# Attention, top-1 experts and a rational-activation MLP on one core: building the token table in two passes

## The chip, the cores and the metric

The kernel runs on one core of a Trainium2 chip. The metric is the time of one execution in device microseconds, from the first to the last instruction of that core and what lies around it. The engines are TensorE (PE), VectorE (DVE), ScalarE (ACT), GpSimd (POOL) and SyncE (SP), each with its own queue; SP and POOL issue the DMAs of the stretch that matters here.

## The reference, cut to what matters

```
x   = linear_attention(q, k, v)            # (8, 8, 576, 64) -> tokens N = 4608, D = 512
keep = x @ w_skip > 0                       # other tokens pass unchanged
e    = argmax(x[keep] @ w_gate)             # one of 8 experts per kept token
g    = softmax(x[keep] @ w_gate)[e]
x[keep] += g * (relu(x[keep] @ w1[e]) @ w2[e])       # w1: 512 x 1024, w2: 1024 x 512
h   = x @ w_in                              # w_in: 512 x 2048, w_out: 2048 x 512
out = P(h) / Q(h) @ w_out                   # cubic over quadratic in |h|, elementwise
```

## The kernel before

There are three stages. Attention (`attention`, eight batches) writes the tokens to `xd` in DRAM and keeps the router's logits in SBUF. The experts (`experts`) read them, and `mlp` does the last two products in blocks of 384 tokens. Products in float32 are made of three passes over a high and a low half, so weights and activations are first split: ScalarE copies the high half, VectorE or GpSimd subtracts to get the low one.

The experts work in up to 25 slots of 256 tokens, each slot of one expert; a slot has two halves of 128, so there are `NH` = 50 columns of token indices `sidx` (128 x 50), one per half. The change lies in how `sidx` comes about and who waits for it.

`positions` gives every token a place. `token_table` (L696) turns places into `sidx` in four chunks of 12, 12, 8 and 4 token columns. In each chunk VectorE compares (`hh`, which of the 50 columns), compares (`lh`, which of the 128 rows) and multiplies by the token number (`tg`); PE adds a matmul for each token column into the PSUM tile `ptab`. Two more VectorE instructions (`high`, `sidx`) finish all 50 columns. After the first chunk `slot_table` finds the expert of each slot (`etab`), and SP issues the four loads of the first expert's `w1`. After the table `kind_table` says for each slot how many halves have tokens and whether the next slot has another expert (`kind`, `change`).

Then, in program order (L985 to L996): POOL gathers slot 0's rows (`gather(0)`, two indirect DMAs), issues two loads of `w2`, and gathers slot 1's rows (`gather(1)`). VectorE and ScalarE split the first four of `w1`'s eight column groups, `gate_sum` and `gate_out` store the last tokens' gates to `gd` (many small pieces), PE transposes slot 0's rows, these are split, then the rest of `w1`.

A slot (L911) runs under a branch on `kind`. Slot 0 first splits `w2` (ScalarE the high halves, VectorE and GpSimd in turn the low ones) and gathers its gates. In `part1_full` (L885) PE does layer 1 in four blocks `f2` of 24 matmuls; ScalarE and VectorE make `hh` and `hl` of each (`relu`). In slot 0 `tables()` follows: `next_table`, the loads of the next expert's weights, `pair_table`. PE goes on with the transposes of the next slot's rows and with layer 2 of half 1, whose result is scaled, added and scattered back. After the branch come `gather(i + 2)` and layer 2 of half 0.

Instructions of one engine run in the order of its queue. That order is the code's within each block written with `manual_schedule`; between blocks the compiler may bring work forward (it does so with `gather(2)` in slot 0), but not into or out of a branch that it depends on.

Of the kernel before, what the change touches and what calls it, by code (L numbers as in the profile page):

```python
# [10 lines left out]
I32 = mybir.dt.int32  # L11
# [47 lines left out]
@with_exitstack  # L59
def tile_attention_moe_moe2(ctx: ExitStack, tc: tile.TileContext, q, k, v, w_skip, w_gate, w1, w2, w_in, w_out, ca, cb, out, dbg=None):  # L60
    nc = tc.nc
    nc.scalar.preload_act_table_set("natural_log_exp_and_others")
    const = ctx.enter_context(tc.tile_pool(name="const", bufs=1))
    ident = const.tile([P, P], F32, name="ident")
    make_identity(nc, ident)
    ones = const.tile([P, 2], F32, name="ones")
    nc.vector.memset(ones, 1.0)
    wg = const.tile([P, 4, E + 1], F32, name="wg")
    av = const.tile([P, 4], F32, name="av")
    bv = const.tile([P, 2], F32, name="bv")  # L70
    ab = const.tile([P, 2], F32, name="ab")
    qc = const.tile([P, 1], F32, name="qc")
    nc.vector.memset(qc, 1.0 + 1e-6)
    sidx = const.tile([P, NH], I32, name="sidx")
    gates = const.tile([P, NH], F32, name="gates")
    etab = const.tile([1, 32], I32, name="etab")
    xtab = const.tile([1, 32], I32, name="xtab")
    kind = const.tile([1, 32], I32, name="kind")
    change = const.tile([1, 32], I32, name="change")
    pair = const.tile([1, 3, 32], I32, name="pair")  # L80
    early = const.tile([1, 33], I32, name="early")
    xd = tc.dram_tile([NT, DM], F32, name="xd")
    gd = tc.dram_tile([NT, 1], F32, name="gd")
    wc_in = tc.dram_tile([DM, F2], F32, name="wc_in")
    wc_out = tc.dram_tile([F2, DM], F32, name="wc_out")

    with ExitStack() as rst:
        rc = rst.enter_context(tc.tile_pool(name="r_const", bufs=1))
        logits = rc.tile([P, NC, E + 1], F32, name="logits")
        R = dict(pair=pair, early=early) | routing_tiles(rc)  # L90
        attention(tc, q, k, v, w_gate, w_skip, ca, cb, ident, ones, wg, av, bv, ab, logits, xd, gd, R)
        if dbg is not None and "logits" in dbg:
            nc.sync.dma_start(out=dbg["logits"], in_=logits)
            nc.sync.dma_start(out=dbg["xd"], in_=xd)
            return
        with tc.tile_pool(name="hold", bufs=1, side="right", reuse_waits="tile") as hp:
            hold = hp.tile([P, DM // P * F1], F32, name="hold")
            hs = ExitStack()
            ahead = []
            experts(tc, w1, w2, w_in, w_out, wc_in, wc_out, xd, gd, ident, logits, sidx, gates, etab, xtab, kind, change, pair, early, hold, ahead, hs, R, dbg)  # L100
            if dbg is not None and "sidx" in dbg:
                return
            rst.close()
            if dbg is not None and "x2" in dbg:
                nc.sync.dma_start(out=dbg["x2"], in_=xd)
                nc.sync.dma_start(out=dbg["wi"], in_=wc_in)
                nc.sync.dma_start(out=dbg["wo"], in_=wc_out)
                return
            mlp(tc, xd, wc_in, wc_out, av, ab, qc, ident, hold, ahead, out)
            hs.close()  # L110
# [62 lines left out]
def attention(tc, q, k, v, w_gate, w_skip, ca, cb, ident, ones, wg, av, bv, ab, logits, xd, gd, R):  # L173
    nc = tc.nc
    with ExitStack() as st:
        inp = st.enter_context(tc.tile_pool(name="a_in", bufs=3))
        tails = st.enter_context(tc.tile_pool(name="a_tail", bufs=3))
        work = st.enter_context(tc.tile_pool(name="a_work", bufs=2))
# [209 lines left out]

        def tn(b, j):
            if j == 0:  # L390
                T["xs", b] = work.tile([P, J, DM], F32, name="xs")
            if j == J:
                T["xt", b] = work.tile([P, DM], F32, name="xt")
            xout = T["xs", b][:, j, :] if j < J else T["xt", b]
            if j in ON_ACT and b < B - 1:
                for g in range(H):
                    nc.scalar.activation(xout[:, g * D:(g + 1) * D], T["px", b, j][:, g // 2, (g % 2) * D:(g % 2 + 1) * D], AF.Identity, scale=T["rq", b][:, j, g // 2, g % 2:g % 2 + 1])
                return
            nc.vector.tensor_tensor(out=xout.rearrange("p (r h d) -> p r h d", r=4, h=2), in0=T["px", b, j][:, :, 0:2 * D].rearrange("p r (h d) -> p r h d", h=2),
                                    in1=T["rq", b][:, j].unsqueeze(3).to_broadcast([P, 4, 2, D]), op=ALU.mult)  # L400
# [292 lines left out]
    nc.vector.tensor_copy(out=pair[:, 0], in_=done[:, 1, 32:64])  # L693


def token_table(tc, p, ps, R, sidx):  # L696
    nc = tc.nc
    tok, posb = R["tok"], R["posb"]
    lh = p.tile([P, P, NC], BF16, name="lh")
    ptab = ps.tile([P, 2, NH], F32, name="ptab")  # L700
    c0 = 0
    for n in (CG, CG, 8, 4):
        cs = slice(c0, c0 + n)
        hh = p.tile([P, CG, NH], BF16, name="hh", bufs=2)[:, 0:n]
        tg = p.tile([P, CG, 2, NH], BF16, name="tg", bufs=2)[:, 0:n]
        nc.vector.tensor_tensor(out=hh, in0=R["rowh"].unsqueeze(1).to_broadcast([P, n, NH]), in1=posb[:, 1, cs].unsqueeze(2).to_broadcast([P, n, NH]), op=ALU.is_equal)
        nc.vector.tensor_tensor(out=lh[:, :, cs], in0=R["rowx"][:, :, 0:n], in1=posb[:, 0, cs].unsqueeze(1).to_broadcast([P, P, n]), op=ALU.is_equal)
        nc.vector.tensor_tensor(out=tg, in0=hh.unsqueeze(2).to_broadcast([P, n, 2, NH]),
                                in1=tok.rearrange("p m c -> p c m")[:, cs].unsqueeze(3).to_broadcast([P, n, 2, NH]), op=ALU.mult)
        for c in range(c0, c0 + n):  # L710
            nc.tensor.matmul(out=ptab, lhsT=lh[:, :, c], rhs=tg[:, c - c0], start=(c == 0), stop=(c == NC - 1))
        c0 += n
        yield
    high = p.tile([P, NH], F32, name="high")
    nc.vector.tensor_scalar(out=high, in0=ptab[:, 0, :], scalar1=64.0, scalar2=float(NOWHERE), op0=ALU.mult, op1=ALU.add)
    nc.vector.tensor_tensor(out=sidx, in0=high, in1=ptab[:, 1, :], op=ALU.add)
    yield


def experts(tc, w1, w2, w_in, w_out, wc_in, wc_out, xd, gd, ident, logits, sidx, gates, etab, xtab, kind, change, pair, early, hold, ahead, hs, R, dbg=None):  # L720
    nc = tc.nc
    KD, KF = DM // P, F1 // P
    ET = mybir.EngineType
# [2 lines left out]
    with ExitStack() as st:  # L726
# [151 lines left out]
            load_w2(e)  # L878

        def tables():  # L880
            next_table(tc, R, xtab)
            load_next(0)
            pair_table(tc, R, sidx, change, pair, early)

        def part1_full(i, hh, hl):  # L885
            for f2 in range(KF // 2):
                relu(f2, layer1(i, f2), hh, hl)
            if i == 0:
                tables()
            pts = [transposes(i + 1, a) for a in range(2)] if i < MAXS - 1 else []  # L890
            py = layer2(1, hh, hl)
            for a, pt in enumerate(pts):
# [3 lines left out]
        def part1_half(i, hh, hl):  # L896
            last = i == MAXS - 1
            r = []
            for g in range(2):
                r.append(layer1_half(i, g))  # L900
            pts = []
            for g in range(2):
                split_half(g, turn_half(g, r[g]), hh, hl)
# [1 line left out]
                    pts.append(transposes(i + 1, g))  # L905
            for a, pt in enumerate(pts):
                split_x(i + 1, a, pt)
            if i == 0:
                tables()

        def slot(i, kd, ch):  # L911
            last = i == MAXS - 1
# [10 lines left out]
            with full.Else():  # L923
                with tc.manual_schedule():
                    part1_half(i, hh, hl)
            with tc.manual_schedule():
                if i + 2 < MAXS:
                    gather(i + 2)
# [33 lines left out]
        with tc.manual_schedule():  # L962
# [6 lines left out]
            gate_exp(tc, R, c1, NC)  # L969
            with tc.tile_pool(name="r_ps", bufs=1, space=PSUM, reuse_waits="tile") as rps:  # L970
                positions(tc, rps, R)
                tt = token_table(tc, rp, rps, R, sidx)
                next(tt)
                slot_table(tc, R, etab)
                e0 = expert(etab, 0, [ET.SP, ET.Pool])
                for c in range(4):
                    load_w1(e0, c=c, n=4)
                for _ in range(4):
                    next(tt)
                kind_table(tc, R, sidx, kind, change)  # L980
            pp = st.enter_context(tc.tile_pool(name="e_ps", bufs=1, space=PSUM, reuse_waits="tile"))
            ps["t"] = [pp.tile([P, KD, P], F32, name=f"pt{a}") for a in range(2)]
            ps["h"] = [pp.tile([P, 2 * SLOT], F32, name=f"ph{f2}") for f2 in range(KF // 2)]
# [1 line left out]
            gather(0)  # L985
            for c in range(2):
                load_w2(e0, nc.gpsimd, c, 2)
            gather(1)
            for c in range(W1A):
                split_w1(c, False)  # L990
            gate_sum(tc, R, c1, NC)
            gate_out(tc, R, gd, (B // 2 - 1,))
            for a in range(2):
                split_x(0, a, transposes(0, a))
            for c in range(W1A, 8):
                split_w1(c, False)  # L996
            if dbg is not None and "sidx" in dbg:
                next_table(tc, R, xtab)
                for nm, t in (("sidx", sidx), ("etab", etab), ("kind", kind[:, 0:MAXS]), ("xtab", xtab)):
                    nc.sync.dma_start(out=dbg[nm], in_=t)  # L1000
                return
        with tc.manual_schedule():
            kd, ch = get(kind, 0, 2), get(change, 0, 2)
        with tc.If(kd > 0):
            slot(0, kd, ch)
        rs.close()
        ap_ = hs.enter_context(tc.tile_pool(name="ahead", bufs=1, side="right", reuse_waits="tile"))
        ahead.extend(ap_.tile([P, KD, AHEAD * P], F32R, name=f"wi{m}") for m in "hl")
# [205 lines left out]
```

## Time and profile before

| | |
|---|---|
| Time, median of 3 runs (lowest, highest) | 1399.22 us (1395.91, 1400.88) |
| The profiled execution, its span | 1394.98 us, 1393.3 us |
| PE, PE weight loads | busy 1320.0 us (95%), 1195.8 us (86%) |
| DVE, ACT, POOL | busy 1099.6 us (79%), 890.4 us (64%), 296.5 us (21%) |
| Attention | up to about 153 us |
| Routing and slot 0's rows | about 153 to 181 us |
| Experts, from layer 1 of slot 0 | about 181 to 550 us |
| MLP | from about 567 us |

Busy time is the time in which an engine executes; an engine that is busy 95% of the span leaves little room, but only in the stages where it is. The timeline lists the instructions of an engine in order of time, with the idle time just before each in brackets and what ended it; neighbours of one kind are merged (x4 means four of them). "PEclk" is the TensorE clock that was granted, as a share of full speed.

### The profile page before, as it was taken

Reading aid. Unit: us, or ns where it says so; the run is one execution under the profiler, and the core shown is the slowest. Engines: PE = TensorE matmul, PEld = TensorE weight load, DVE = VectorE, ACT = ScalarE, POOL = GpSimd, SP = SyncE. Lnnn points to the kernel's source line nnn. Section 1 sums busy time; section 2 is a strip of 40 time slices with the busy share of each in tenths; the row PEclk is TensorE's granted clock in tenths of the full one; section 3 lists DMA queues with packets and bytes.
Section 4 is the critical chain, followed back from the end, with each engine's and each line's share of the span. In section 5 each row is a group of like instructions: output and inputs, shape, how many; then the busy total and the mean of one; then the engine's idle time right before and its main releaser. Section 6 shows DMA issues by size and latency. Waiting matters only on the chain.

```text
span 1393.3 us, 22173 instructions
## 1 busy us (share of the span) xinstructions
PE 1320.0 (95%) x7470; PEld 1195.8 (86%) x7470; DVE 1099.6 (79%) x2093; ACT 890.4 (64%) x1726; POOL 296.5 (21%) x247
## 2 busy tenths in 40 slices
PE   4999489999899999799999999999999999999998
PEld 3989378888898898789999999999999999999997
DVE  6998754764646565699888888888888888888887
ACT  2655235544242422699787878787877787878786
POOL 5756044556343452241000000000000000000000
PEclk9999689999999999899999999999999999999999
DMA  9984455667646654421000000000000000000000
GB/s 280 320 277 145 129 131 198 230 220 260 229 151 232 239 179 147 139 91 61 23 23 24 23 24 23 23 24 23 24 23 23 24 23 24 23 24 24 1 23 23
DMA packets 86929, 143.82 MB, mean 103 GB/s; under 512 B 21925, under 2 KB 52645, under 8 KB 85745
## 3 DMA queue, kind: packets, MB, share of 16 engines
q1 hardware_dynamic: 79696, 125.88, 27.1%
q0 software_dynamic: 7072, 16.06, 3.8%
q8 instruction: 70, 1.15, 0.4%
q14 instruction: 91, 0.74, 0.2%
HBM read 110.66 MB, written 35.15 MB: 105 GB/s over the span
## 4 chain that ended last, share of the span: by engine, by line
PE 55%; DVE 2%; issue 1%; ACT 1%; DMA 1%; POOL 0%; POOLq 0%; ACTq 0%; DVEq 0%
PE ph L1106 27%; PE py L1151 27%; DMA xd<-y,sidx 1%; PE pt L1090 1%; DVE gl L1132 0%; DVE qq L1130 0%; DVE r L1134 0%; DVE qq L1136 0%; DVE pn L1140 0%; DVE pn L1138 0%; ACT qq L1121 0%; ACT m L1119 0%; DVE pn L1141 0%; POOL x L792 0%; ACT gh L1115 0%
## 5 line engine op out<-in xcount | busy, mean ns | idle before, releaser
L1151 PE MATMUL py<-woh,gl 128*128 128x512 f32 x576 | 227.5, 395 | 0.1
L1151 PE MATMUL py<-woh,gh 128*128 128x512 f32 x576 | 227.4, 395 | 0.0
L1151 PE MATMUL py<-wol,gh 128*128 128x512 f32 x576 | 226.9, 394 | 0.0
L1115 ACT CAST gh<-pn 128x384 fp32r<-128x384 f32 x192 | 98.7, 514 | 142.5 <-PE py L1151 137.2
L1132 DVE TENSOR_TENSOR gl<-pn,gh 128x384 fp32r<-128x384 f32 x192 | 110.1, 573 | 69.5 <-ACT gh L1115 69.3
L1121 ACT ACTIVATE qq<-m,ab 128x384 f32<-128x384 f32 x192 | 136.4, 711 | 6.4
L1106 PE MATMUL ph<-xh,wi0h 128*128 128x384 f32 x384 | 129.6, 338 | 0.3 <-DVE pn L1141 0.2
L1106 PE MATMUL ph<-xh,wi0l 128*128 128x384 f32 x384 | 129.7, 338 | 0.0
L1106 PE MATMUL ph<-xl,wi0h 128*128 128x384 f32 x384 | 129.0, 336 | 0.0
L1151 PEld LDWEIGHTS py<-woh,gl 128*128 128x128 f32 x576 | 108.0, 188 | 24.4 <-DVE gl L1132 1.2
L813 PE MATMUL ph<-xth,w1h 128*128 128x256 f32 x416 | 120.4, 289 | 6.8 <-ACT cvs L743 6.0
L1123 ACT ACTIVATE pn<-ph,av 128x384 f32<-128x384 f32 x192 | 125.5, 653 | 0.0
L1141 DVE SCALAR_TENSOR_TENSOR pn<-pn,av,ph 128x384 f32<-128x384 f32 x192 | 118.1, 615 | 6.8
L1151 PEld LDWEIGHTS py<-wol,gh 128*128 128x128 f32 x576 | 108.2, 188 | 17.8
L1151 PEld LDWEIGHTS py<-woh,gh 128*128 128x128 f32 x576 | 108.3, 188 | 17.5 <-ACT gh L1115 0.6
L1136 DVE TENSOR_TENSOR qq<-m,qq 128x384 f32<-128x384 f32 x192 | 106.8, 556 | 17.7 <-issue 3.9
L813 PE MATMUL ph<-xtl,w1h 128*128 128x256 f32 x416 | 120.0, 288 | 0.1
L813 PE MATMUL ph<-xth,w1l 128*128 128x256 f32 x416 | 119.8, 288 | 0.0
L1138 DVE SCALAR_TENSOR_TENSOR pn<-pn,av,r 128x384 f32<-128x384 f32 x192 | 117.3, 611 | 0.1
L1126 ACT ACTIVATE r<-qq,qc 128x384 f32<-128x384 f32 x192 | 115.9, 604 | 0.0
L1130 DVE SCALAR_TENSOR_TENSOR qq<-qq,r 128x384 f32<-128x384 f32 x192 | 108.7, 566 | 0.0
L1134 DVE SCALAR_TENSOR_TENSOR r<-qq,r 128x384 f32<-128x384 f32 x192 | 106.9, 557 | 0.0
(231 smaller groups left out, 3225.1 us busy)
## 6 DMA issues: line engine op xcount, KB each, us to landing
hold<-in_moe_w_dram SPq DMA_DIRECT2D x8, 2048.0 KB
w2s<-in_moe_w_dram SPq DMA_DIRECT2D x8, 2048.0 KB
hold<-xd SPq DMA_DIRECT2D x12, 768.0 KB
out_dram<-o SPq DMA_DIRECT2D x36, 256.0 KB
vm<-in_v_dram SPq DMA_DIRECT2D x8, 1024.0 KB
qm<-in_q_dram SPq DMA_DIRECT2D x8, 1024.0 KB
xd<-xs SPq DMA_DIRECT2D x8, 1024.0 KB
raw<-in_moe_w_in_dram SPq DMA_DIRECT2D x16, 512.0 KB
```

The lines of the kernel that those rows point to most:

```text
L813: nc.tensor.matmul(out=ph[:, u, :], lhsT=a[:, k, fs], rhs=b[:, k, :], start=(n == 0), stop=(n == 3 * KD - 1))
L1106: nc.tensor.matmul(out=ph, lhsT=w[:, k, :], rhs=x[:, k, :], start=(n == 0), stop=(n == 3 * KD - 1))
L1121: nc.scalar.activation(qq, m, AF.Identity, scale=ab[:, 1:2], bias=ab[:, 0:1])
L1123: nc.scalar.activation(pn, ph, AF.Identity, scale=av[:, 3:4], bias=av[:, 2:3])
L1126: nc.scalar.activation(r2, T[("q",) + second], AF.Ln, bias=qc)
L1130: nc.vector.scalar_tensor_tensor(out=q3, in0=q3, scalar=1.0 + 1e-6, in1=r3, op0=ALU.add, op1=ALU.mult)
L1132: GL(nc).tensor_tensor(out=gl, in0=pn4, in1=gh.bitcast(F32), op=ALU.subtract)
L1134: nc.vector.scalar_tensor_tensor(out=r3, in0=q3, scalar=2.0, in1=r3, op0=ALU.subtract, op1=ALU.mult, reverse0=True)
L1136: nc.vector.tensor_tensor(out=qq, in0=m, in1=qq, op=ALU.mult)
L1138: nc.vector.scalar_tensor_tensor(out=p3, in0=p3, scalar=av[:, 0:1], in1=r3, op0=ALU.add, op1=ALU.mult)
L1141: nc.vector.scalar_tensor_tensor(out=pn, in0=pn, scalar=av[:, 1:2], in1=ph, op0=ALU.add, op1=ALU.mult)
L1151: nc.tensor.matmul(out=py, lhsT=g[:, ts_], rhs=w[:, f, :], start=(f == 0 and n == 0), stop=(f == KF - 1 and n == 2))
```

## The change

Columns 0 and 1 (slot 0) get a pass of their own through all four chunks. `token_table` becomes `table_part` (one chunk for the columns h0 to h1) and `table_end`. The first pass runs before `slot_table`; `first_kind` finds slot 0's `kind` from its two columns. For the other 48 columns, chunks 0 and 1 stand behind the issue of slot 0's gather and of `w2`, ahead of `gate_sum`; chunks 2 and 3 stand in `tables()`, with `gather(1)` and `kind_table` behind them. `tables()` moves from behind all four blocks of layer 1 to behind the second (f2 == 1). Their sums go to the PSUM tile of layer 2's half 0. `lh` is made once, in the first pass. Slot 0's `change` is read behind its branch. Two column groups of `w1` instead of four are split before slot 0's rows. In attention the output tiles `xs` and `xt` move to a pool of their own, allocated first.

```diff
 def attention(...)
+        res = st.enter_context(tc.tile_pool(name="a_res", bufs=2))
...
-                T["xs", b] = work.tile([P, J, DM], F32, name="xs")
+                T["xs", b] = res.tile([P, J, DM], F32, name="xs")
...
-                T["xt", b] = work.tile([P, DM], F32, name="xt")
+                T["xt", b] = res.tile([P, DM], F32, name="xt")
...
+CHUNKS = (CG, CG, 8, 4)
+
+def table_part(nc, p, R, lh, ptab, m, h0, h1):
+    tok, posb = R["tok"], R["posb"]
+    nh, c0, n = h1 - h0, sum(CHUNKS[:m]), CHUNKS[m]
+    cs = slice(c0, c0 + n)
+    hh = p.tile([P, CG, nh], BF16, name=f"hh{h0}", bufs=2)[:, 0:n]
+    tg = p.tile([P, CG, 2, nh], BF16, name=f"tg{h0}", bufs=2)[:, 0:n]
+    nc.vector.tensor_tensor(out=hh, in0=R["rowh"][:, h0:h1].unsqueeze(1).to_broadcast([P, n, nh]), in1=posb[:, 1, cs].unsqueeze(2).to_broadcast([P, n, nh]), op=ALU.is_equal)
+    nc.vector.tensor_tensor(out=tg, in0=hh.unsqueeze(2).to_broadcast([P, n, 2, nh]),
+                            in1=tok.rearrange("p m c -> p c m")[:, cs].unsqueeze(3).to_broadcast([P, n, 2, nh]), op=ALU.mult)
+    if h0 == 0:
         nc.vector.tensor_tensor(out=lh[:, :, cs], in0=R["rowx"][:, :, 0:n], in1=posb[:, 0, cs].unsqueeze(1).to_broadcast([P, P, n]), op=ALU.is_equal)
+    for c in range(c0, c0 + n):
+        nc.tensor.matmul(out=ptab, lhsT=lh[:, :, c], rhs=tg[:, c - c0], start=(c == 0), stop=(c == NC - 1))
+
+def table_end(nc, p, ptab, sidx, h0, h1):
+    high = p.tile([P, h1 - h0], F32, name=f"high{h0}")
     nc.vector.tensor_scalar(out=high, in0=ptab[:, 0, :], scalar1=64.0, scalar2=float(NOWHERE), op0=ALU.mult, op1=ALU.add)
+    nc.vector.tensor_tensor(out=sidx[:, h0:h1], in0=high, in1=ptab[:, 1, :], op=ALU.add)
+
+def first_kind(tc, R, sidx, kind0):
+    nc = tc.nc
+    occ = R["occ"][:, 0:2]
+    nc.vector.tensor_scalar(out=occ, in0=sidx[0:1, 0:2], scalar1=float(NT), scalar2=None, op0=ALU.is_lt)
+    nc.vector.tensor_tensor(out=kind0, in0=occ[:, 0:1], in1=occ[:, 1:2], op=ALU.add)
...
         def tables():
+            for m in range(2, len(CHUNKS)):
+                table_part(nc, rest["p"], R, rest["lh"], rest["ptab"], m, 2, NH)
+            table_end(nc, rest["p"], rest["ptab"], sidx, 2, NH)
+            gather(1)
+            kind_table(tc, R, sidx, kind, change)
             next_table(tc, R, xtab)
...
                 relu(f2, layer1(i, f2), hh, hl)
-            if i == 0:
-                tables()
+                if i == 0 and f2 == 1:
+                    tables()
...
                     part1_half(i, hh, hl)
+            if i == 0:
+                ch = get(change, 0, 2)
...
                 positions(tc, rps, R)
-                tt = token_table(tc, rp, rps, R, sidx)
-                next(tt)
+                lh = rp.tile([P, P, NC], BF16, name="lh")
+                ptab = rps.tile([P, 2, 2], F32, name="ptab")
+                for m in range(len(CHUNKS)):
+                    table_part(nc, rp, R, lh, ptab, m, 0, 2)
                 slot_table(tc, R, etab)
+                table_end(nc, rp, ptab, sidx, 0, 2)
                 e0 = expert(etab, 0, [ET.SP, ET.Pool])
                 for c in range(4):
                     load_w1(e0, c=c, n=4)
-                for _ in range(4):
-                    next(tt)
-                kind_table(tc, R, sidx, kind, change)
+                first_kind(tc, R, sidx, kind0)
...
             gather(0)
             for c in range(2):
                 load_w2(e0, nc.gpsimd, c, 2)
-            gather(1)
-            for c in range(W1A):
-                split_w1(c, False)
+            rest = dict(p=rp, lh=lh, ptab=ps["y"][0][:, 0:2 * (NH - 2)].rearrange("p (m h) -> p m h", m=2))
+            for m in range(2):
+                table_part(nc, rp, R, lh, rest["ptab"], m, 2, NH)
             gate_sum(tc, R, c1, NC)
             gate_out(tc, R, gd, (B // 2 - 1,))
+            for c in range(W1A // 2):
+                split_w1(c, False)
             for a in range(2):
                 split_x(0, a, transposes(0, a))
-            for c in range(W1A, 8):
+            for c in range(W1A // 2, 8):
                 split_w1(c, False)
+            nc.vector.memset(kind, 0)
...
-            kd, ch = get(kind, 0, 2), get(change, 0, 2)
+            kd = get(kind0, 0, 2)
```

In `part1_half`, which a slot of one filled half takes, `tables()` moves ahead of the second transposes in the same way.

## Rows read from the trace of the kernel before

**Rows 1.** Timeline of VectorE: start us, us, engine line op out<-in, idle before.
```profile
158.41 0.78 DVE L706 TENSOR_TENSOR hh<-r_rowh,r_posb 128x600 bf16<-128x600 bf16 x1
161.28 0.96 DVE L707 TENSOR_TENSOR lh<-r_rowx,r_posb 128x1536 bf16<-128x1536 bf16 x1 [2.10 <-DMA xd<-xt]
162.16 1.40 DVE L708 TENSOR_TENSOR tg<-hh,r_tok 128x1200 bf16<-128x1200 bf16 x1
163.47 0.41 DVE L650 TENSOR_TENSOR r_cand<-r_rows,r_cum 1x256 f32<-1x256 f32 x1
...
164.55 0.77 DVE L706 TENSOR_TENSOR hh<-r_rowh,r_posb 128x600 bf16<-128x600 bf16 x1
...
167.43 0.56 DVE L706 TENSOR_TENSOR hh<-r_rowh,r_posb 128x400 bf16<-128x400 bf16 x1
167.92 0.67 DVE L707 TENSOR_TENSOR lh<-r_rowx,r_posb 128x1024 bf16<-128x1024 bf16 x1
168.52 0.97 DVE L708 TENSOR_TENSOR tg<-hh,r_tok 128x800 bf16<-128x800 bf16 x1
...
169.70 0.41 DVE L707 TENSOR_TENSOR lh<-r_rowx,r_posb 128x512 bf16<-128x512 bf16 x1
170.03 0.56 DVE L708 TENSOR_TENSOR tg<-hh,r_tok 128x400 bf16<-128x400 bf16 x1
...
171.42 0.21 DVE L716 TENSOR_TENSOR sidx<-high,ptab 128x50 int32<-128x50 f32 x1
```

**Rows 2.** Timeline of GpSimd, gathers and loads ahead of slot 0 and in it.
```profile
172.51 1.53 POOL L792 DMA_INDIRECT x<-xd,sidx  x1 [34.82 <-DMA hold<-in_moe_w_dram]
174.34 1.28 POOL L792 DMA_INDIRECT x<-xd,sidx  x1 [0.30 <-issue]
175.63 1.62 POOL L775 DMA_DIRECT2D w2s<-in_moe_w_dram  x2
...
191.13 1.10 POOL L873 DMA_INDIRECT gates<-gd,sidx  x1 [11.16 <-DMA gd<-r_gate]
...
196.16 5.02 POOL L780 TENSOR_TENSOR w2l<-w2s,w2h 128x512 fp32r<-128x512 f32 x4
```

**Rows 3.** Timeline of TensorE, transposes, layer 1 and layer 2 of slot 0.
```profile
178.96 1.11 PE L798 MATMUL pt<-ident,x 128*128 128x128 f32 x4 [1.08 <-DMA x<-xd,sidx]
180.74 0.58 PE L813 MATMUL ph<-xth,w1h 128*128 128x256 f32 x1 [0.68 <-ACT xth L778]
...
187.18 0.28 PE L813 MATMUL ph<-xth,w1h 128*128 128x256 f32 x1
...
196.24 0.48 PE L829 MATMUL py<-w2h,hh 128*128 128x512 f32 x1
```

**Rows 4.** Timeline of SyncE's queue, the DMAs that it issues.
```profile
146.31 1.30 SPq L610 DMA_DIRECT2D gd<-r_gate  x2
...
153.46 0.34 SPq L409 DMA_DIRECT2D xd<-xs  x1
...
165.36 2.12 SPq L770 DMA_DIRECT2D hold<-in_moe_w_dram  x4
175.37 0.37 SPq L608 DMA_DIRECT2D gd<-r_gate  x1
...
203.71 0.38 SPq L770 DMA_DIRECT2D hold<-in_moe_w_dram  x1
```

**Rows 5.** Windows: stretch, its us, busy us (x instructions), PEclk granted, DMA share, GB/s.
```profile
168.00:170.00 2.00, 1.17 (x15) 1.10 (x14) 2.00 (x4) 0.99 (x2) 0.00 (x0) 0.50 1.07 349
```

**Rows 6.** Timeline of ScalarE, the copies of the second half of w2.
```profile
192.56 2.18 ACT L778 CAST w2h<-w2s 128x512 fp32r<-128x512 f32 x4 [0.42 <-DMA w2s<-in_moe_w_dram]
```

**Rows 7.** Timeline of VectorE inside slot 0.
```profile
195.34 1.89 DVE L820 SCALAR_TENSOR_TENSOR hl<-ph,hh 128x512 fp32r<-128x512 f32 x3 [0.39 <-issue]
...
198.26 3.20 DVE L660 SCALAR_TENSOR_TENSOR r_cand<-r_cand,r_cum 1x256 f32<-1x256 f32 x1
...
201.94 0.41 DVE L662 TENSOR_TENSOR r_cand<-r_nend,r_cum 1x256 f32<-1x256 f32 x1
```

More of the change, by code (lines that the diff above doesn't have):

```diff
@@ L79, in tile_attention_moe_moe2 @@
     change = const.tile([1, 32], I32, name="change")
+    kind0 = const.tile([1, 1], I32, name="kind0")
     pair = const.tile([1, 3, 32], I32, name="pair")
@@ L99, in tile_attention_moe_moe2 @@
             ahead = []
-            experts(tc, w1, w2, w_in, w_out, wc_in, wc_out, xd, gd, ident, logits, sidx, gates, etab, xtab, kind, change, pair, early, hold, ahead, hs, R, dbg)
+            experts(tc, w1, w2, w_in, w_out, wc_in, wc_out, xd, gd, ident, logits, sidx, gates, etab, xtab, kind0, kind, change, pair, early, hold, ahead, hs, R, dbg)
             if dbg is not None and "sidx" in dbg:
@@ L693, in pair_table @@
     nc.vector.tensor_copy(out=pair[:, 0], in_=done[:, 1, 32:64])
-def token_table(tc, p, ps, R, sidx):
-    nc = tc.nc
[L698 to L717, printed above, removed]
@@ L720, in experts @@
-def experts(tc, w1, w2, w_in, w_out, wc_in, wc_out, xd, gd, ident, logits, sidx, gates, etab, xtab, kind, change, pair, early, hold, ahead, hs, R, dbg=None):
+CHUNKS = (CG, CG, 8, 4)
[9 more added lines that the diff above has]
+    if h0 == 0:
+        nc.vector.tensor_tensor(out=lh[:, :, cs], in0=R["rowx"][:, :, 0:n], in1=posb[:, 0, cs].unsqueeze(1).to_broadcast([P, P, n]), op=ALU.is_equal)
+    for c in range(c0, c0 + n):
+        nc.tensor.matmul(out=ptab, lhsT=lh[:, :, c], rhs=tg[:, c - c0], start=(c == 0), stop=(c == NC - 1))
@@ new lines, in table_end @@
+def table_end(nc, p, ptab, sidx, h0, h1):
+    high = p.tile([P, h1 - h0], F32, name=f"high{h0}")
+    nc.vector.tensor_scalar(out=high, in0=ptab[:, 0, :], scalar1=64.0, scalar2=float(NOWHERE), op0=ALU.mult, op1=ALU.add)
+    nc.vector.tensor_tensor(out=sidx[:, h0:h1], in0=high, in1=ptab[:, 1, :], op=ALU.add)
+def first_kind(tc, R, sidx, kind0):
+    nc = tc.nc
+    occ = R["occ"][:, 0:2]
+    nc.vector.tensor_scalar(out=occ, in0=sidx[0:1, 0:2], scalar1=float(NT), scalar2=None, op0=ALU.is_lt)
+    nc.vector.tensor_tensor(out=kind0, in0=occ[:, 0:1], in1=occ[:, 1:2], op=ALU.add)
@@ L721, in experts @@
+def experts(tc, w1, w2, w_in, w_out, wc_in, wc_out, xd, gd, ident, logits, sidx, gates, etab, xtab, kind0, kind, change, pair, early, hold, ahead, hs, R, dbg=None):
     nc = tc.nc
@@ L900, in part1_half @@
                 r.append(layer1_half(i, g))
+            if i == 0:
+                tables()
             pts = []
@@ L907, in part1_half @@
                 split_x(i + 1, a, pt)
-            if i == 0:
-                tables()
         def slot(i, kd, ch):
@@ L925, in slot @@
                     part1_half(i, hh, hl)
+            if i == 0:
+                ch = get(change, 0, 2)
             with tc.manual_schedule():
@@ L1002, in experts @@
         with tc.manual_schedule():
-            kd, ch = get(kind, 0, 2), get(change, 0, 2)
+            kd = get(kind0, 0, 2)
         with tc.If(kd > 0):
-            slot(0, kd, ch)
+            slot(0, kd, None)
         rs.close()
```

## The prediction

> **What bounds the kernel now.** I read the busy table first (TensorE, here PE, is busy 95% of the span), then the timeline of each engine over the handover from attention to the experts, because the change lies there alone. On VectorE (DVE) the reader sees one chain: the token table runs from 158.41 to the token indices `sidx`, ready at 171.42 + 0.21 = 171.63 us; inside it stand a 2.10 us wait of `lh` for the store of `xt`, and four pairs of comparison and product over all 50 columns [rows 1]. GpSimd (POOL) then gathers slot 0's rows and only after that issues the two loads of `w2` [rows 2]. PE transposes the second half of those rows at 178.96 and begins layer 1 of slot 0 at 180.74 [rows 3]. From there PE hardly stops until the end of the experts: what reaches it late in slot 0 makes the end late. At 196.24 it starts the first layer 2 of slot 0 (half 1). This is the point at which I compare, because after it PE's order of work is the same in both kernels.
>
> **The first pass (two columns).** Two columns replace fifty in eight instructions (`hh` and `tg`, four chunks). None of that width is in the trace; the nearest row is an instruction of 128x50 elements, 0.21 us (`sidx`), the wide bound is the 0.56 us of the smallest `tg`, 128x400 [rows 1]. I take 0.21: the new ones have at most 48 elements. Eight make 1.7 us. The four `lh` stay, at their distance to the next instruction: 0.88 twice, 0.60 and 0.33, 2.7 us. The 2.10 us wait should go, since `xs` and `xt` move to a pool of their own and `lh` no longer lies on them. 158.41 + 4.4 = 162.8. `slot_table` now follows (163.47 to 164.55, 1.08 us) and hides the last matmuls; two more of 0.21 give sidx of slot 0 at 164.3, that is 7.3 us earlier, or 4.5 at the wide bound. The 36 narrow matmuls run on an idle PE. `first_kind` adds two more, 0.4 us: 164.7. The loads of `w1` start 1.89 after `slot_table` begins [rows 1, 4], at 164.7 instead of 165.36.
>
> **The gathers and weights ahead of slot 0.** The first gather starts 0.88 us after sidx (171.63 to 172.51), the second 1.83 later, the `w2` loads 1.29 after that [rows 2]: 165.2, 167.0, 168.3. PE gets the second half of the rows 4.62 us after its gather starts (174.34 to 178.96) and layer 1 begins 1.78 later [rows 2, 3]: 171.6 and 173.4. The rows now share the DMA engines with `w1`, which moved 349 GB/s alone [rows 5]; half a megabyte more is 1.5 us at that rate, the upper bound. I take 173.9, a head start of 6.8 us. The rest pass over chunks 0 and 1 lies beside the fetch: on DVE twice 0.78 + 1.31 from 164.7 to 168.9, and PE's matmuls behind that have 2.7 us before the rows are there, so it costs nothing; without that cover it would be 4.2 us. `gate_sum` (three instructions at 0.21) ends at 169.6, and the small stores to `gd` issue there instead of at 175.37 [rows 4].
>
> **The table inside slot 0.** This is where I see the gain go. Four things stand ahead of it in program order.
> - PE: layer 1 blocks f2 = 0 and 1 are 48 matmuls. Before, from 187.18 to 196.24 PE ran 68 of layer 1's 96 matmuls and 8 transposes, 0.12 us each; the other 28, from 180.74 to 187.18, took 6.44 us, because the granted clock still stood at the lower of its two levels (1.2 GHz), to which it had fallen while PE had little to do; it was 0.50 at 168 to 170, too [rows 3, 5]. So f2 = 1 ends at 173.9 + 6.4 + 2.4 = 182.7. Then come the twelve table matmuls of chunks 2 and 3, and behind them f2 = 2: PE must wait for DVE, which it never did before.
> - DVE: the table stands behind the halves of `split_w2` and behind `hl` of f2 = 0 and 1. The w2l instructions wait for ScalarE's copies and these for `w2`. Before, the second half of `w2` was there at 192.56, 16.9 us after the issue at 175.63 [rows 2, 6], and the second `hl` was done 4.0 later (195.34 + two thirds of 1.89) [rows 7]. With issue at 168.3: 185.2 and 189.3. If `w2` came at once, the second `hl` would still need f2 = 1, a copy and a subtraction of some 0.63 each: 184.0.
> - The table's own work, from the first `hh` of chunk 2 to sidx, is 171.63 - 167.43 less the two `lh` (0.60, 0.33) = 3.3 us [rows 1], and PE is released two instructions (0.4) before its end.
> - POOL: the gather of slot 1's rows moves from ahead of slot 0 to behind the two gate gathers (half of the 5.03 us from 191.13 to 196.16) and the four w2l (5.02 us) [rows 2]. The gate gathers wait for `gd`. They began 15.8 us after its store was issued (175.37 to 191.13) [rows 2, 4]; at that delay they begin at 185.5 and the w2l run from 188.0 to 193.0. The low bound is the 7.15 us that SP, with a `gd` store issued at 146.31, waited for it before its next store at 153.46 [rows 4]: gate gathers from 176.8, and POOL holds nothing up.
>
> Then DVE and POOL meet. At 198.26 an instruction of 256 elements took 3.20 us where the next of its size took 0.41; it began while POOL's w2l ran and ended 0.28 after them (201.18) [rows 2, 7]. The table's `hh` and `tg` likewise read two operands from SBUF, so I let them wait until 193.0. The Trainium skill (SBUF — State Buffer, "Who interferes with whom") says more than that row: any DVE instruction with two SBUF inputs is blocked fully by a GpSimd instruction that reads SBUF, whichever came first holding the port. By it the `tensor_tensor` forms of the table are subject to it; without it the sum is the second rival's.
>
> Sum: 193.0 + 3.3 = sidx at 196.3, PE goes on at 195.9 after 13 us of waiting. Gather at 197.2, its second half at 199.0, rows there 4.62 later at 203.6, the last transposes 0.5: layer 2 of half 1 starts at 204.1 instead of 196.24, **7.9 us later**. Layer 1's last 48 matmuls lie beside the gather, at 5.8 us, or 8.8 if the idle PE fell to the lower clock again [rows 3]; the second makes it 205.6, up to 9.4 later. I take 7.8.
>
> Costed at nothing: `gather(2)` now stands behind the branch, but its rows are needed only a whole layer 1 and two layers 2 later; without that cover it costs its 6 us. The next expert's loads stand behind nine small instructions after sidx; they were issued at 203.71 [rows 4], 7.4 us after the new sidx, which is room enough for those at 0.21 to 0.41 each. The reads of `change` on five queues are done while PE has matmuls queued, else 0.3 us. `memset(kind)` is one small DVE instruction on idle time.
>
> **The time.** The profiled execution took 1394.98 us (span 1393.3 and 1.7 around it), 4.24 less than the median 1399.22 of three. Nothing behind the compared point is limited by anything but the work before it, so the shift stays whole: 1402.8 against the profiled execution, 1407.0 against the median. A measurement tells about 0.3%, 4.2 us, from no change.
>
> **Rivals.**
> 1. *`w2` and `gd` arrive early; only the order costs.* All of `w1`, slot 0's rows and `w2`, 4.6 MB at 349 GB/s [rows 5], would be in 13.2 us after 164.7, at 177.9. Then `hl` at 184.0 rules, sidx 187.3, gathers 188.2 and 190.0, rows 194.6, layer 2 at 195.1: 1.1 us earlier, 1398.1. For it: the `gd` bound above. Against it: `w2` alone took 16.9 us before. The Trainium skill (DMA: Bandwidth & Descriptors, "Queues, rings and completion order") says that a DMA engine takes turns between its queues packet by packet, so POOL's `w2` need not wait for SP's `w1`; an argument for this rival that no row here shows. Chance 0.24.
> 2. *No blocking between DVE and POOL, but POOL's queue holds the gather.* Table from 189.3, sidx 192.6, but POOL is free at 193.0: gathers 193.0 and 194.8, rows 199.4, layer 2 at 199.9: 3.7 later, 1402.9. Chance 0.18.
> 3. *Faster: the table runs ahead of the split of `w2` in DVE's queue.* The queues don't follow the listing everywhere: POOL gathered slot 2's rows between 191.13 and 196.16 [rows 2], ahead of w2l that stand before it in the code. If DVE's first `hh` of chunk 2 begins before the second half of `w2` has landed, neither DVE nor POOL holds the gather, and the head start of 6.8 stays whole: 1392.4. Against it: the table stands inside the branch on `kd`, behind which no queue jumped in the trace. Chance 0.08.
> 4. *Later still:* the `gd` stores queue behind `w1` on SP's queue. `w1` and slot 0's rows, 2.6 MB at 349 GB/s, last from 164.7 to 172.2, 2.5 us past the issue of `gd` at 169.7; gates, w2l and table shift by that: 1409.5. Chance 0.07.
>
> The forecast itself has 0.43. **Faster** by over 0.3% is rival 3, 0.08. **Same** is rival 1 and more than half of rival 2, 0.34. **Slower** is the forecast, rival 4 and the rest, 0.58. The range reaches from rival 1 less 2 us of run-to-run spread, 1396, to 1411, between rival 4 and the forecast with the lower clock and that spread; the forecast's own range is 1404 to 1410.
>
> **What would show it.** Right: sidx's first two columns near 164.3 and no wait on `lh`; layer 1 near 174; a hole on PE of 5 to 13 us between f2 = 1 and 2, ended by DVE's `tg`; a `tg` or `hh` of several us ending with POOL's w2l; the gather of slot 1's rows behind w2l. Wrong: no hole on PE, or the second layer-1 half unbroken, or slot 1's transposes before 195.

## The result and the profile after

The changed kernel takes 1407.19 us (median of 5 runs, 1404.52 to 1408.49) where the kernel before takes 1397.91 beside it (5 runs): a ratio of 1.0066, 95% interval 1.0038 to 1.0093. It is slower. The prediction said 1407.0; it added a shift of 7.8 us to an earlier median of 1399.22, and the shift measured here is 9.28 on 1397.91. So it is luck that the two times agree to 0.2 us. The profiled executions took 1404.52 and 1394.98 us, so they are 9.54 apart.

VectorE first (start us, us, engine, line, operation, tiles). The first `lh` starts without a wait, and slot 0's two columns are ready at 164.41. Inside slot 0 one `w2l` takes 6.04 us where the others take 0.69, and `hh` of chunk 2 stands behind it [rows 1, 7].

```profile
159.25 0.95 DVE L711 TENSOR_TENSOR lh<-r_rowx,r_posb 128x1536 bf16<-128x1536 bf16 x1
...
164.25 0.16 DVE L719 TENSOR_TENSOR sidx<-high,ptab 128x2 int32<-128x2 f32 x1
...
186.30 0.69 DVE L789 TENSOR_TENSOR w2l<-w2s,w2h 128x512 fp32r<-128x512 f32 x1 [0.90 <-ACT w2h L787]
187.34 6.04 DVE L789 TENSOR_TENSOR w2l<-w2s,w2h 128x512 fp32r<-128x512 f32 x1 [0.35 <-ACT w2h L787]
193.31 1.27 DVE L829 SCALAR_TENSOR_TENSOR hl<-ph,hh 128x512 fp32r<-128x512 f32 x2
194.51 0.54 DVE L707 TENSOR_TENSOR hh<-r_rowh,r_posb 128x384 bf16<-128x384 bf16 x1
...
197.72 0.20 DVE L719 TENSOR_TENSOR sidx<-high,py 128x48 int32<-128x48 f32 x1
```

GpSimd's queue: slot 0's gathers are 6 to 7 us earlier than before, slot 1's have moved behind the gates and the four w2l, which run from 187.92 to 192.83 [rows 2].

```profile
165.88 2.06 POOL L801 DMA_INDIRECT x<-xd,sidx  x1 [26.40 <-DVE hh L707]
168.23 1.55 POOL L801 DMA_INDIRECT x<-xd,sidx  x1 [0.30 <-issue]
169.78 1.62 POOL L784 DMA_DIRECT2D w2s<-in_moe_w_dram  x2
184.94 1.41 POOL L882 DMA_INDIRECT gates<-gd,sidx  x1 [13.54 <-DMA gd<-r_gate]
...
187.92 4.91 POOL L789 TENSOR_TENSOR w2l<-w2s,w2h 128x512 fp32r<-128x512 f32 x4
198.68 1.19 POOL L801 DMA_INDIRECT x<-xd,sidx  x1 [5.85 <-DVE change L676]
```

TensorE: layer 1 starts at 178.39, only 2.35 us earlier than before. It stops for 8.94 us until DVE's `tg`, and the first layer 2 (half 1) starts at 205.54 instead of 196.24 [rows 3]. The transposes at 204.75 follow the last matmul without a wait.

```profile
176.60 1.11 PE L807 MATMUL pt<-ident,x 128*128 128x128 f32 x4 [1.15 <-DMA x<-xd,sidx]
178.39 0.58 PE L822 MATMUL ph<-xth,w1h 128*128 128x256 f32 x1 [0.68 <-ACT xth L787]
...
196.09 1.34 PE L713 MATMUL py<-tg,lh 128*128 128x96 bf16 x12 [8.94 <-DVE tg L708]
197.22 0.56 PE L822 MATMUL ph<-xth,w1h 128*128 128x256 f32 x1
...
204.75 1.03 PE L807 MATMUL pt<-ident,x 128*128 128x128 f32 x8
205.54 0.47 PE L838 MATMUL py<-w2h,hh 128*128 128x512 f32 x1
```

The windows (columns as in [rows 5]; the third number from the end is the granted clock) show two more things. After the rows are in, the DMA engines move little though w2 is not there yet, and behind the hole, in which PE did nothing for 8.94 us, the granted clock is 0.50, the lower of its two levels (1.2 GHz), until 200.

```profile
178.00:180.00 2.00, 1.46 (x5) 1.17 (x6) 1.63 (x3) 2.00 (x5) 0.00 (x0) 0.50 1.60 174
180.00:182.00 2.00, 2.00 (x11) 2.00 (x11) 2.00 (x5) 1.45 (x3) 0.00 (x0) 0.50 0.64 47
...
192.00:194.00 2.00, 0.00 (x0) 0.00 (x0) 2.00 (x3) 0.00 (x0) 0.83 (x1) 0.50 0.00 0
...
198.00:200.00 2.00, 2.00 (x11) 2.00 (x11) 1.83 (x8) 0.00 (x0) 1.19 (x1) 0.50 0.00 0
```

### The profile page after: what moved, and what is told of

The parts are those of the page before. It is cut to its first block, busy times and chain, and to the rows that moved or that the text cites. A ratio compares the mean times of both kernels' runs of the same rounds, so it can differ in the third digit from the quotient of the medians.

```text
span 1402.9 us, 22254 instructions
## 1 busy us (share of the span) xinstructions
PE 1328.9 (95%) x7506; PEld 1202.9 (86%) x7506; DVE 1108.8 (79%) x2106; ACT 890.0 (63%) x1726; POOL 302.7 (22%) x247
## 4 chain that ended last, share of the span: by engine, by line
PE 55%; DMA 3%; DVE 2%; ACT 2%; issue 1%; POOL 0%; POOLq 0%; ACTq 0%
PE ph L1126 27%; PE py L1171 27%; DMA xd<-y,sidx 3%; PE pt L1110 1%; DVE gl L1152 0%; DVE qq L1150 0%; ACT qq L1141 0%; DVE pn L1158 0%; ACT pn L1143 0%; DVE qq L1156 0%; ACT m L1139 0%; ACT gh L1135 0%; ACT r L1146 0%; DVE pn L1160 0%; DVE r L1154 0%
```

## The experiments

Attention ends up to 4 us earlier or later from one execution to the next, so the stages are counted from the first `hh` of the table in each profile. "Layer 1" and "layer 2" are the first matmul of each in slot 0, in the one profiled execution. Medians are of all runs of a kernel (5 in before and changed, 6 to 12 in e1 to e10, one in e11 and e12); ratios, with 95% intervals, are to the kernel before, run beside each group (medians of 1397.95 to 1398.19 beside e1 to e10).

| kernel | layer 1 | layer 2 | median us | ratio |
|---|---|---|---|---|
| before | 22.33 | 37.83 | 1397.91 | |
| changed | 19.48 | 46.63 | 1407.19 | 1.0066 (1.0038 to 1.0093) |
| e1, the pool alone | 20.10 | 35.04 | 1393.62 | 0.9962 (0.9942 to 0.9981) |
| e2, w2l on DVE | 18.45 | 41.00 | 1402.39 | 1.0023 (1.0003 to 1.0042) |
| e3, rest ahead | 18.57 | 32.98 | 1395.71 | 0.9980 (0.9964 to 0.9996) |
| e4, gates late | 18.06 | 43.34 | 1406.83 | 1.0056 (1.0032 to 1.0081) |
| e5, rows first | 18.03 | 48.37 | 1409.48 | 1.0089 (1.0060 to 1.0118) |
| e6, table in the gap | 16.81 | 40.80 | 1402.90 | 1.0034 (1.0016 to 1.0053) |
| e7, ahead and rows first | 17.99 | 32.90 | 1401.54 | 1.0020 (0.9998 to 1.0043) |
| e8, e3 with e2 and e4 | 18.51 | 32.99 | 1395.88 | 0.9973 (0.9955 to 0.9992) |
| e9, pool, gates late | 19.97 | 34.99 | 1395.17 | 0.9965 (0.9946 to 0.9984) |
| e10, the pool again | 19.98 | 34.87 | 1394.41 | 0.9964 (0.9944 to 0.9983) |
| e11, before again | 25.44 | 39.82 | 1396.31 | |
| e12, changed again | 18.42 | 44.44 | 1405.81 | |

**e1: before, with `xs` and `xt` in a pool of their own** (the `a_res` lines of the change and nothing else).

> The kernel before, with only the move of xs and xt to a pool of their own. Theory: the 2.10 us wait of the first lh goes, all behind it comes 2.1 us earlier (sidx 169.5, layer 1 at 178.6, layer 2 of slot 0 at 194.1), and the time falls by 2 us to about 1396 against a median of 1398 for the kernel before, which a comparison cannot tell from no change. Rival: the second half of w2 lands at 192.6 as before, since the loads are not held by their issue, and layer 2 starts at 196.2 as before: no gain at all.

The first `lh` follows `hh` at once (159.95 behind 159.26). Layer 2 came 2.8 us earlier; the second half of w2 arrived at 189.54 and so did not stay where it was, as the rival had it. The median fell by 4.6, more than the 2.10 us of the wait. Timeline of VectorE:

```profile
159.26 0.78 DVE L707 TENSOR_TENSOR hh<-r_rowh,r_posb 128x600 bf16<-128x600 bf16 x1
159.95 0.95 DVE L708 TENSOR_TENSOR lh<-r_rowx,r_posb 128x1536 bf16<-128x1536 bf16 x1
```

**e2: the four w2l of POOL on DVE.**

```diff
-                        split_w2(f)
+                        split_w2(f, False)    # slot 0: all eight on DVE
```

> The changed kernel, with slot 0's four w2l of POOL on DVE, so nothing of POOL's reads SBUF beside DVE. Theory (the hole on PE is set by DVE's w2l held behind POOL's four): the 6.04 us w2l becomes 0.69, all eight w2l end near 189, the table's hh of chunk 2 starts near 190 instead of 194.5, PE's hole ends near 193 instead of 197.2, slot 1's rows are gathered from 195 instead of 198.7, layer 2 starts at 199.6 to 201.2 instead of 205.5, and the time is 1401 to 1403 where the changed kernel has 1407. Rival (the late data of w2 and gd set it): hh of chunk 2 stays at 194 or later, layer 2 at 205, time 1407.

No w2l is held, all eight take 5.1 us together, and PE's hole shrinks from 8.94 to 5.21. From the first `hh` the table's `hh` of chunk 2 is at 30.2 instead of 35.6 and layer 2 at 41.0 instead of 46.6. So the held w2l is some 5.6 us of the loss in that profile. Against the second profile of the changed kernel (e12, layer 2 at 44.44) it is 3.4, and the medians differ by 4.8. Timeline of VectorE:

```profile
188.81 2.50 DVE L789 TENSOR_TENSOR w2l<-w2s,w2h 128x512 fp32r<-128x512 f32 x4 [0.91 <-ACT w2h L787]
191.22 1.28 DVE L829 SCALAR_TENSOR_TENSOR hl<-ph,hh 128x512 fp32r<-128x512 f32 x2
192.42 0.55 DVE L707 TENSOR_TENSOR hh<-r_rowh,r_posb 128x384 bf16<-128x384 bf16 x1
```

**e3: the part inside slot 0 undone.**

```diff
-            for m in range(2):
+            for m in range(len(CHUNKS)):
                 table_part(nc, rp, R, lh, rest["ptab"], m, 2, NH)
+            table_end(...); gather(1); kind_table(...)     # no longer in tables()
```

> The changed kernel, with chunks 2 and 3 of the rest pass, its end, the gather of slot 1's rows and kind_table ahead of slot 0, behind chunks 0 and 1 (only the part inside slot 0 is undone). Theory (the hole on PE and the gather behind it are the whole loss): no hole, layer 1 from 178.4 without a break to 193, layer 2 between 193.5 and 197, held by w2l and hl rather than by PE; time 1396 to 1399, as the kernel before, and not 5 us better, since the head start of layer 1 is only 2.4 us. Rival (the late rows, weights and gate stores cost as much by themselves: the gd store now issues 3.6 us later still): layer 2 not before 200, time above 1402.

No hole; layer 2 starts at 33.0, earlier than before and than forecast, and waits once, 0.52 us, for POOL's w2l. The table's place in slot 0 is thus the whole loss: with the rest of the change kept, the kernel is a little faster than before. The edit also makes the gate stores later (174.29 instead of 169.53), and w2 is then copied without a break from 181.01; e4 moves these stores without the table and gains no time. Timeline of TensorE:

```profile
192.46 0.48 PE L838 MATMUL py<-w2h,hh 128*128 128x512 f32 x1
...
194.14 0.50 PE L838 MATMUL py<-w2l,hh 128*128 128x512 f32 x1 [0.52 <-POOL w2l L789]
```

**e4: the gate stores behind the split of w2, the gathers of the gates behind the table.**

```diff
-            gate_sum(tc, R, c1, NC); gate_out(tc, R, gd, ...)    # ahead of split_w1
+                    gate_sum(...); gate_out(...)                 # slot 0, behind split_w2
```

> The changed kernel, with slot 0's gate_sum and the small gd stores behind the split of w2 in slot 0, and the gathers of its gates behind the table and the gather of slot 1's rows. Theory (the 16-byte and 4-byte stores to gd hold up the w2 loads that are under way): without them both halves of w2 have landed by 181, POOL's w2l run from 182 to 187, layer 2 starts at 198 to 199.5, time 1399 to 1401. Rival (w2 is late for another reason): the copies of its second half start at 185.7 as now, w2l on POOL end at 189.5, layer 2 at 201 to 202, time 1403.

The copies of both halves of w2 run without a break from 180.24, right behind ScalarE's w1 (183.01 and 185.65 in the changed kernel), so w2 did wait for the small stores. The gain is lost again: POOL's w2l now run together with DVE's, four of DVE's take 6.85 us, and slot 1's rows make PE wait 1.37 us. Layer 2 started at 202.56, 3 to 4.5 us later than expected. The time, 1406.8, is 6 to 8 above what the theory said. In the profiles, the stretch from layer 2 to the MLP's first transposes takes 367.79 us against 364.63 in the changed kernel, so what layer 2 gained is lost again there; why is open. Timelines of ScalarE, VectorE and GpSimd:

```profile
180.24 4.26 ACT L787 CAST w2h<-w2s 128x512 fp32r<-128x512 f32 x8
...
181.52 6.85 DVE L789 TENSOR_TENSOR w2l<-w2s,w2h 128x512 fp32r<-128x512 f32 x4
...
181.46 6.36 POOL L789 TENSOR_TENSOR w2l<-w2s,w2h 128x512 fp32r<-128x512 f32 x4 [9.75 <-ACT w2h L787]
```

**e5: three quarters of w1 behind slot 0's rows.**

```diff
-                for c in range(4):
-                    load_w1(e0, c=c, n=4)
+                load_w1(e0, c=0, n=4)    # c = 1 to 3 on ACT's queue, behind the copies of c = 0
```

> The changed kernel, with only the first quarter of w1 loaded ahead of the gather of slot 0's rows; the other three quarters are issued on ACT's queue behind the copies of the first. Theory (the rows came late because w1's 2 MB were under way): counted from the first hh of the table, layer 1 of slot 0 starts at 15.5 to 17 us instead of 19.5 (18.1 and 18.5 in the two runs that kept this part of the change). The time stays at 1405 to 1409, since the hole on PE still ends with DVE's table. Rival (the gather itself is that slow): layer 1 at 18 or later, as now.

Half a miss. The first 128 rows, with little else under way, were at PE 4.78 us after their gather started (165.53 on POOL), where the changed kernel took 8.48. The second half, fetched while w1's other quarters were, took 6.93 (from 167.89), and layer 1 needs both. W1's last quarter is copied only at 187.63, and the hole grows to 13.12 us. Timeline of TensorE:

```profile
170.31 1.08 PE L807 MATMUL pt<-ident,x 128*128 128x128 f32 x4 [0.57 <-DMA x<-xd,sidx]
174.82 1.11 PE L807 MATMUL pt<-ident,x 128*128 128x128 f32 x4 [3.43 <-DMA x<-xd,sidx]
```

**e6: every part where nothing seemed to wait for it** (e5's order of loads; `hh` and `tg` of chunks 2 and 3 ahead of layer 1, their matmuls behind f2 = 0; the split of w2, gate stores and gate gathers behind the gather of slot 1's rows).

> All parts put where the runs so far say that nothing waits: w1's first quarter, then slot 0's rows, then the rest of w1; DVE makes hh and tg of all four chunks ahead of layer 1; PE sums chunks 2 and 3 behind the first block of layer 1 (f2 = 0); the split of w2, the gate stores and the gathers of the gates come behind the gather of slot 1's rows. Theory (PE's start and the hole are all that counts): no hole over 1 us, layer 1 starts 15.5 to 17 us after the first hh and layer 2 31 to 33 us after it (37.8 before, 46.6 changed, 35.0 with the pool alone), time 1390 to 1394. Rival (weights are late: w1's later quarters or w2 now arrive behind PE's need): PE waits for DMA between the blocks, layer 2 at 35 or later, time 1395 or more.

The rival's numbers held, but not its wait: PE stops for rows, not for weights. Layer 1 starts at 16.8 and PE runs through the table without a hole, but w1's last quarter, issued behind w2, arrives at 186.63. ScalarE's copies and DVE's subtractions of it stand ahead of `sidx`, which is ready at 190.81. Slot 1's rows are gathered at 193.43, while the gate stores are under way, and PE waits 7.16 us for them. Timeline of TensorE:

```profile
200.97 1.97 PE L815 MATMUL pt<-ident,x 128*128 128x128 f32 x8 [7.16 <-DMA x<-xd,sidx]
```

**e7: e3 and e5 together.**

> The run with the whole rest pass ahead of slot 0 and, as well, three quarters of w1 issued behind slot 0's rows. Theory (rows late because of w1): layer 1 at 16.5 to 17.5 us after the first hh instead of 18.6, held by DVE's own queue, layer 2 at 31.5 instead of 33.0, time 1 to 2 us below the 1395.7 of that run, which a comparison cannot tell from it. Rival: layer 1 at 18.6 as in that run.

Layer 1 came at 18.0, between the 16.5 to 17.5 of the theory and the 18.6 of the rival, and layer 2 at 32.9, no earlier than in e3; then layer 2 itself waits 1.50 us for POOL's w2l and 4.72 for `hl`. In `tables()` a `tensor_tensor` of 256 elements had met POOL's w2l (193.38, 4.96 us), and two `hl` were queued behind it. Timeline of VectorE:

```profile
193.32 5.30 DVE L664 TENSOR_TENSOR r_cand<-r_nend,r_cum 1x256 f32<-1x256 f32 x1
...
201.26 1.27 DVE L829 SCALAR_TENSOR_TENSOR hl<-ph,hh 128x512 fp32r<-128x512 f32 x2
```

**e8: e3 with e2's and e4's edits.**

> The run with the whole rest pass ahead of slot 0, and with it both covers that the other runs gave: all eight w2l of slot 0 on DVE, the gate stores behind them and the gathers of the gates behind the tables. Theory: layer 1 starts 18.0 to 18.6 us after the first hh as there, runs without a break, layer 2 starts at 32.5 to 33.0 with no wait for w2l (0.52 there); time 1394 to 1396, 0.5 to 1.5 below that run's 1395.7. Rival (later slots take the rest back, since they wait for other things): layer 2 as early, time 1396 or above.

Layer 2 at 33.0 with no wait, but 1395.88: no better than e3. The rival is right that the rest is taken back, and a part of it goes in slot 0 already: the gates now come late, VectorE stands 9.57 us until they let it make the first `y`, and PE waits 1.80 us for that `y`. Timelines of VectorE and TensorE:

```profile
207.16 0.75 DVE L845 SCALAR_TENSOR_TENSOR y<-py,gates,x 128x512 f32<-128x512 f32 x1 [9.57 <-DMA gates<-gd,sidx]
...
207.97 0.39 PE L822 MATMUL ph<-xtl,w1h 128*128 128x256 f32 x1 [1.80 <-DVE y L845]
```

**e9: e1 with e4's edit. e10: e1 once more.**

> The kernel before with xs and xt in a pool of their own, and slot 0's gate stores behind the split of w2, the gathers of its gates behind the tables. Theory (the small gd stores hold up w2): the copies of w2's second half start at most 11 us after the first issue of w2 (15.1 us in the run with the pool alone, 16.9 before); layer 2 starts at 35 us after the first hh as with the pool alone, since PE's own work sets it there; time 1393 to 1395. Rival (w2 takes that long by itself): the copies start 15 us after the issue as well.

> The run with the pool alone once more, beside the two others on one chip. If its gain is real, the ratio to the kernel before is again 0.994 to 0.998 (0.9962 the first time), where the wait it removes is worth 0.9985; if the first ratio was luck, it is 0.998 to 1.000.

The two differ only in where slot 0's gates are stored and gathered. With the stores late the copies of w2's second half start 10.6 us after its first issue (173.81 to 184.43), with them in their old place 16.1 (174.22 to 190.33). Windows of e9, then of e10:

```profile
180.00:182.00 2.00, 2.00 (x12) 2.00 (x10) 1.78 (x4) 1.61 (x4) 1.30 (x1) 0.50 0.97 363
182.00:184.00 2.00, 2.00 (x11) 2.00 (x11) 1.89 (x2) 1.14 (x3) 1.82 (x2) 0.53 0.74 275
```

```profile
180.00:182.00 2.00, 2.00 (x11) 2.00 (x11) 2.00 (x4) 0.99 (x2) 0.00 (x0) 0.50 1.37 111
182.00:184.00 2.00, 2.00 (x11) 2.00 (x11) 0.04 (x1) 0.00 (x0) 0.00 (x0) 0.50 0.47 66
```

The small stores hold up w2, but with the pool alone PE sets layer 2 at 35.0 in both, and the times agree. e10 repeats e1's gain. Its profiled execution took 1401.37 us, e1's 1392.69, and the rows show two reasons. DVE's last w2l met POOL's four, which cost PE 4.15 us; in e1 it was done before they began. Much later PE waits 5.99 us for `cvs`, a scratch tile of ScalarE's, where e1 waits 0.5; e1 has one wait of 3.49 us nearby that e10 lacks. Timelines of VectorE and TensorE in e10:

```profile
192.03 6.04 DVE L781 TENSOR_TENSOR w2l<-w2s,w2h 128x512 fp32r<-128x512 f32 x1 [0.35 <-ACT w2h L779]
197.99 2.47 DVE L821 SCALAR_TENSOR_TENSOR hl<-ph,hh 128x512 fp32r<-128x512 f32 x4
...
198.72 0.79 PE L830 MATMUL py<-w2h,hl 128*128 128x512 f32 x1 [4.15 <-DVE hl L821]
...
357.58 0.58 PE L814 MATMUL ph<-xth,w1h 128*128 128x256 f32 x1 [5.99 <-ACT cvs L744]
```

**e11 and e12: before and changed, one more profile of each.**

> The kernel before, unchanged, profiled once more, since the pool alone gained 5 us at the median where the wait it removes took 2.1. Theory (the profiled execution of before was a lucky one, 3 us under its median): here lh waits longer than 2.1 us for the store of xt, or DVE's last w2l is held beside POOL's four for about 6 us as in the second run of the pool alone, and the time is above 1397. Rival: the same rows as before, wait 2.1, no held w2l; then the rest of the gain stays unexplained.

> The changed kernel, unchanged, profiled once more. Theory (the hole is built into the order): DVE's last w2l is again held until POOL's four are done, PE's hole is 9 to 11 us, layer 2 starts 45 to 48 us after the first hh (46.6 the first time). Rival (the hole of the first profile was one execution's bad luck): w2l not held, layer 2 at 41 to 42 us as in the run with w2l on DVE.

In e11 `lh` waited 5.24 us instead of 2.10, and no w2l was held; the time, 1396.31, is just under the 1397 I had set. The wait that the pool removes varies, and that fits a gain of more than 2.1 us at the median; two draws don't show it, since e11 began layer 2 3.92 us later than the first profile of before and ended only 1.33 later. In e12 (1405.81 us) a w2l is held again; the hole of 8.83 and layer 2 at 44.4 are just under what I had set. One row of VectorE from e11, then one from e12:

```profile
166.36 0.96 DVE L707 TENSOR_TENSOR lh<-r_rowx,r_posb 128x1536 bf16<-128x1536 bf16 x1 [5.24 <-DMA xd<-xt]
```

```profile
186.76 5.21 DVE L789 TENSOR_TENSOR w2l<-w2s,w2h 128x512 fp32r<-128x512 f32 x2 [2.15 <-ACT w2h L787]
```

## Why the prediction was right, and which of its steps were not

| step | predicted | measured |
|---|---|---|
| slot 0's columns ready | 164.3 | 164.41 |
| first gather, w2 issued | 165.2, 168.3 | 165.88, 169.78 |
| layer 1 starts | 173.9 | 178.39 |
| second half of w2 there | 185.2 | 185.65 |
| gathers of the gates | 185.5 | 184.94 |
| POOL's w2l | 188.0 to 193.0 | 187.92 to 192.83 |
| hole on PE | 13 us | 8.94 us |
| sidx of the other slots | 196.3 | 197.92 |
| layer 2 starts | 204.1, up to 205.6 | 205.54 |

**Right: the chain that sets the end.** It runs from the gate stores over POOL's queue (gate gathers, then w2l) to a held DVE instruction, from there to the table and to PE. e2 takes one link out and gets 3.4 to 5.6 us back; e3 takes the table off it and gets all back. e4 takes the gate stores out and gets layer 2 only 3.3 us earlier (1.1 against e12), and no time, since the two engines then meet sooner. Rival 2, without the blocking, falls with the 6.04 us of one w2l and with POOL, which was free at 192.83 and then waited 5.85 us for DVE. Rival 1 needed w2 and `gd` early; the second half of w2 was copied from 185.65 and the gate gathers began at 184.94, both near the forecast. Its low bound for `gd` was misread besides: of the 7.15 us from 146.31 to 153.46 SP waited 2.2 for a store to `gd`, and it had issued six more such stores in between. Rival 3 falls since DVE kept the listed order, rival 4 since the gate gathers were not late. PE waits for no row of slot 2, so `gather(2)` behind the branch cost nothing, as costed.

**Wrong in size: the head start.** The step "PE gets the second half of the rows 4.62 us after its gather starts", with 1.5 us as the bound for sharing with w1, failed: it took 8.37 (168.23 to 176.60). e5 shows that the loads of w1 under way account for it: 4.78 for the half that was ahead of most of them. Half a megabyte at the full rate was no bound, since, as I read it, the rows shared with all of w1's bytes in flight. Counted from the table's start, layer 1 gained 2.85 us; the pool alone gives 2.23 of that (e1). Five microseconds of earlier gathers bought some 0.6 to 2 (e1 against the changed kernel, e2, e4 and e12). It did not move the sum, since the hole ends with DVE's table: PE stood 8.94 us there instead of 13.

**Wrong in the victim: which instruction is held.** I let the table's `hh` and `tg` wait until 193.0. It was the last w2l, one step ahead of them, until 193.38, and the two `hl` (1.2 us) still stood between. That is why sidx came 1.6 later than said. The Trainium skill (SBUF — State Buffer, "Who interferes with whom") has DVE instructions with two SBUF inputs contend with GpSimd's reads; the trace agrees, 6.04 us against 0.69. The prediction took from there that the one which came first holds the port; here the trace differs, since DVE's w2l began first (187.34 against 187.92) and was held all the same.

**Wrong in what is late next.** I had slot 1's rows arrive last (203.6). They were there when PE was: the transposes follow layer 1 without a wait. PE was the later one, with a clock of 0.50 from 192 to 200 behind the hole, so that the last 48 matmuls took 7.5 us (197.22 to 204.75) and not 5.8. The text had this as its upper case, 205.6.

**The shift stayed whole** here: 9.30 at layer 2, 9.54 at the end. That they agree so well is luck. At the MLP's first transposes the shift is 7.75, and from there to the end of the span the MLP, whose code is the same, takes 830.9 us before and 832.7 after. Timelines of TensorE, before and after (PEq and DVEq are the sequencers of those engines):

```profile
562.42 1.94 PE L1090 MATMUL pt<-ident,hold 128*128 128x128 f32 x8 [7.22 <-PEq L1021]
```

```profile
570.17 1.94 PE L1110 MATMUL pt<-ident,hold 128*128 128x128 f32 x8 [4.29 <-DVEq L1040]
```

Nor is it a rule. e3 starts layer 2 2.1 us earlier than e1, and its median is 2.1 higher; e8 starts 1.9 to 2.0 earlier than e9 and e10, and its median is 0.7 to 1.5 higher. So kernels with the split table seem to lose 2.6 to 4.2 us behind that point. This is not shown: the intervals of the times overlap, and from layer 2 to the MLP's first transposes e1 and e10, one kernel, take 363.00 and 372.27 us, with e3 (364.91) and e8 (369.77) between them.

Before and changed are both beaten by e1 and e10, the move of two tiles alone, at 0.996 of the time before (intervals from 0.994 to 0.998).

## What to carry to other kernels

Before work is moved into a stage, ask what stands ahead of it in each of its queues, and whether one of those can be held by another engine: the table's own work took 3.4 us (194.51 to 197.92), and its place cost 9. An index that is ready earlier brings its rows earlier only if the DMA engines are free by then (e5). And a wait whose length depends on a store in flight is worth removing for itself, since one profile shows one draw of it.

## What the runs showed of the hardware that I had not expected

- A DVE instruction with two SBUF inputs can be held until POOL's whole run of four is over, also if it began first: 187.34 to 193.38 beside POOL's 187.92 to 192.83, in e10 192.03 to 198.07, in e7 193.32 to 198.62 beside 193.38 to 198.34. It isn't always so. In e4 and e5 both engines slow down instead: four of DVE's take 6.85 and 5.72 us where they take 2.5 undisturbed (e2), four of POOL's 6.36 and 6.59 where they otherwise take 4.9, and in e5 DVE is done first. No run shows what decides between the two. Timelines of VectorE and GpSimd in e5:

```profile
189.63 5.72 DVE L789 TENSOR_TENSOR w2l<-w2s,w2h 128x512 fp32r<-128x512 f32 x4
...
189.89 6.59 POOL L789 TENSOR_TENSOR w2l<-w2s,w2h 128x512 fp32r<-128x512 f32 x4 [5.14 <-ACT w2h L787]
```

- Gate stores in pieces of 16 and 4 bytes, issued at about the same time as w2's loads, cut what the DMA engines moved to 66 to 111 GB/s, against 275 to 363 without them (e10 and e9, 180 to 184). In e3 the stores came 3.9 us behind w2, and w2 was copied without a break. The Trainium skill (DMA: Bandwidth & Descriptors, "Specifications") says that a transfer below 512 bytes makes the engine read, modify and write; no run here shows whether that is the reason.
- Two profiles of one kernel can differ by 8.7 us (e1 and e10). The order of two engines' instructions at one place accounts for 4.15 of it; the rest lies further on.
